# Queueing the casts of B and C behind bank copies, and taking two token tiles of the second layer by turns

## The chip, the cores and the metric

The kernel runs on one core of a Trainium2 chip. The metric is the device time of one execution in microseconds (us). Before the change the median of three runs is 602.65 us (601.85 to 606.14). The engines in the text are PE (TensorE, the matrix engine), ACT (ScalarE), DVE (VectorE), POOL (GpSimd) and SP (SyncE, which here only issues DMAs).

## The reference

```
# attention scan: batch 4, 8 heads, 768 positions, head dim 32, state 16
L = exp(cum[i] - cum[j]) * causal           # decay inside a chunk
y = ((C B^T) * L) x + decayed C state       # chunk by chunk, the state carried on
x = y as 3072 tokens x 256
# first layer, d_ff 768
h = max(x @ w1, x @ w2, x @ w3);  x = h @ w_out
# second layer, d_ff 1536
out = (sigmoid(x @ w_gate) * (x @ w_val)) @ w_out
```

x, a, B and C are 32-bit; the weights of both layers are 64-bit floating-point numbers that arrive as integer words and are turned into a hi/lo pair of 32-bit numbers on the chip ("decode").

## The kernel before, in words

**Tiling.** The 3072 tokens are 6 token tiles of 512 (t = 0 to 5). Each of the two layers goes through the tiles, and inside a tile through pieces of 128 hidden columns: 6 (m) in the first layer, 12 in the second. One piece of the first layer is three products `u` (one PSUM bank each, 6 matmuls of 128x512: two k, three terms of a hi/lo split), then the down product `o` of the piece before (6 matmuls into two banks). A piece of the second layer has two products `u` (gate and value) and the down product. So a tile of the first layer is 6 x (18 + 6) = 144 such matmuls and a tile of the second 12 x (12 + 6) = 216. The `u` banks rotate through three PSUM buffers (pool `psu`); a bank is free again when ACT or DVE has read it. In the first layer ACT copies bank 0 (`s`, line 383) and DVE takes the maximum with banks 1 and 2 (385, 387); then ACT casts `hi` (376) and POOL forms `lo` (378). In the second layer ACT forms the sigmoid (392), DVE the product with the value bank (394), ACT `hi`, and POOL (tile 0) or DVE (later tiles) `lo`.

**The attention runs ahead of the first layer.** It is cut into 8 chunks of 96 positions (c), each of 8 steps (g); a step is 4 small products `s` (C times B), a mask by the decay `dec` (`mt`), and 4 products `y`. Its steps are mixed into the first layer's slots (a slot is one `u` bank or one down product): while tile t runs, the steps that tile t + 1 needs are issued: 12 during tile 0, 8 during tile 1, 12 during tile 2, 12 during tile 3, 8 during tile 4, none during tile 5.

**B and C of a chunk** (`split_bc`, for chunks 2 to 7) are loaded as fp32 (`bc`), and split into three bf16 parts p = 0, 1, 2: ACT casts (`parts`, line 239), POOL subtracts (248), and after each cast SP issues DMAs (244; 6, 4 and 2 of them) that copy the part into `bi` and `cs`, from which PE reads. `bc` and `parts` have one buffer each, `bi` and `cs` two. `split_bc(c + 1)` is added to the pipe at the first step of chunk c.

**Weights of the second layer** are decoded in 24 pieces (two for each m: gate and value, 128x512; down, 128x256) during and after tile 5 of the first layer: three ACT operations (136, 138, 139), two on DVE (142, 144), a cast on ACT (148) and a subtraction on POOL (150). `weights_tick` starts one piece in each slot.

**What sets the order.** The code adds work in generators that advance by one stage at each tick, but the tile framework's scheduler then orders the instructions of each engine by its own estimate of when they are ready, so that an instruction can stand earlier in its engine's queue than the code has it. `tc.issue_after(i)` adds an edge for the order alone: what is traced inside it stands behind `i` in that engine's queue, with no wait for `i` to end. Every engine takes its queue in order.

## Time and profile before

| What | Value |
|---|---|
| Median of three runs | 602.65 us (601.85 to 606.14) |
| The profiled execution's own time, its span | 604.28 us, 602.5 us |
| PE busy | 563.0 us, 93% of the span |
| DVE, ACT, POOL busy | 53%, 43%, 31% |
| Last matmul of a `u` or `o` bank ends | about 599 us |

The profile is of one execution. Times inside it count from the span's start. PE's busy time contains overlap: one 128x512 matmul is shown with a length of 389 ns, while in a full stretch the next one starts after some 227 ns; so a tile's length says more than the busy share. A row of a timeline ends with the idle time ahead of the instruction and with what ended it, in brackets.

### The profile page before, as it was taken

To read this page: it belongs to the slowest core of one execution; us is meant where nothing else is said; L and a number is where in the kernel's file an instruction comes from. 1 tells how busy PE (TensorE), PEld (TensorE's weight loads), DVE (VectorE), ACT (ScalarE), POOL (GpSimd) and SP (SyncE) were. 2 spreads that over 40 slices of the span, in tenths; PEclk is the share of its full clock that TensorE was granted. 3 is DMA by queue.
4 is the path that set the end of the run, shared out by engine and by line. 5 is a ranking of instruction groups with operands and counts; after the bars stand their busy time and mean duration, and the time that the engine had idled before them with its cause. 6 is when DMAs were issued, how large, how long until landed. Compare 5 with 4: busy or idle time off the path is not lost.

```text
span 602.5 us, 8006 instructions
## 1 busy us (share of the span) xinstructions
PE 563.0 (93%) x2992; PEld 444.7 (74%) x2992; DVE 317.5 (53%) x467; ACT 260.0 (43%) x475; POOL 186.0 (31%) x207
## 2 busy tenths in 40 slices
PE   5778797997989999999999999999999999999997
PEld 4656575675767777777768888888888888888885
DVE  4899962644745755368987133344344334334332
ACT  5777653224233223279897243233233223223322
POOL 3668874335453424237668210000000000000000
PEclk9859998998999989999999999999999999999999
DMA  7998975373763900099000000000000000000000
GB/s 252 326 313 233 205 183 93 102 132 86 155 134 83 178 28 1 1 316 312 1 2 0 2 35 1 0 1 35 2 0 36 0 1 36 1 1 35 1 0 35
DMA packets 35367, 50.53 MB, mean 84 GB/s; under 512 B 3456, under 2 KB 24320, under 8 KB 35328
## 3 DMA queue, kind: packets, MB, share of 16 engines
q1 hardware_dynamic: 35328, 50.02, 32.0%
q8 instruction: 23, 0.38, 0.3%
q14 instruction: 16, 0.13, 0.1%
HBM read 38.51 MB, written 3.25 MB: 69 GB/s over the span
## 4 chain that ended last, share of the span: by engine, by line
PE 63%; DVE 9%; DMA 8%; ACT 5%; issue 4%; POOL 2%; SPq 1%; DVEq 0%; ACTq 0%; POOLq 0%
PE u L338 14%; PE u L339 14%; PE u L340 14%; PE o L339 7%; PE o L340 6%; PE o L338 6%; DMA cs<-parts 4%; DVE dec L228 2%; DMA dec<-ad 1%; DMA bc<-in_bch 1%; DVE t_b L142 1%; DVE s L387 1%; DVE s L385 1%; PE y L291 1%; POOL lo L378 1%
## 5 line engine op out<-in xcount | busy, mean ns | idle before, releaser
L376 ACT CAST hi<-s 128x512 fp32r<-128x512 f32 x108 | 67.1, 621 | 193.1 <-DVE s L394 153.8
L394 DVE TENSOR_TENSOR s<-u,s 128x512 f32<-128x512 f32 x72 | 49.7, 690 | 126.2 <-PE u L340 125.9
L338 PE MATMUL u<-xt_hi,w_b 128*128 128x512 f32 x288 | 112.4, 390 | 0.8 <-DVE s L385 0.6
L339 PE MATMUL u<-xt_lo,w_b 128*128 128x512 f32 x288 | 112.1, 389 | 0.0
L340 PE MATMUL u<-xt_hi,w_b 128*128 128x512 f32 x288 | 112.1, 389 | 0.0
L338 PE MATMUL u<-xt_hi,w_a 128*128 128x512 f32 x216 | 90.8, 420 | 10.4 <-ACT s L383 5.8
L339 PE MATMUL u<-xt_lo,w_a 128*128 128x512 f32 x216 | 87.2, 404 | 1.8 <-DVE xt_lo L302 1.8
L340 PE MATMUL u<-xt_hi,w_a 128*128 128x512 f32 x216 | 87.0, 403 | 0.0
L378 POOL TENSOR_TENSOR lo<-s,hi 128x512 fp32r<-128x512 f32 x48 | 66.4, 1384 | 64.1 <-ACT hi L376 63.0
L338 PEld LDWEIGHTS u<-xt_hi,w_b 128*128 128x128 f32 x288 | 54.1, 188 | 13.3 <-DVE s L385 1.1
L378 DVE TENSOR_TENSOR lo<-s,hi 128x512 fp32r<-128x512 f32 x60 | 41.5, 692 | 40.6 <-ACT hi L376 40.4
L340 PEld LDWEIGHTS u<-xt_hi,w_b 128*128 128x128 f32 x288 | 54.1, 188 | 11.3
L339 PEld LDWEIGHTS u<-xt_lo,w_b 128*128 128x128 f32 x288 | 54.1, 188 | 11.0
L338 PEld LDWEIGHTS u<-xt_hi,w_a 128*128 128x128 f32 x216 | 42.2, 195 | 25.1 <-ACT s L383 8.0
L228 DVE TENSOR_TENSOR_SCAN dec<-dec,delta 128x388 f32<-128x388 f32 x64 | 57.9, 944 | 3.2 <-DMA dec<-ad 3.0
L339 PE MATMUL o<-lo,w_b 128*128 128x512 f32 x144 | 56.1, 390 | 0.0
L340 PE MATMUL o<-hi,w_b 128*128 128x512 f32 x144 | 56.0, 389 | 0.0
L339 PEld LDWEIGHTS u<-xt_lo,w_a 128*128 128x128 f32 x216 | 42.1, 195 | 10.3 <-DVE xt_lo L302 2.3
L340 PEld LDWEIGHTS u<-xt_hi,w_a 128*128 128x128 f32 x216 | 42.0, 194 | 9.5
L392 ACT ACTIVATE s<-u 128x512 f32<-128x512 f32 x72 | 43.2, 600 | 10.8 <-PE u L340 9.8
L385 DVE TENSOR_TENSOR s<-u,s 128x512 f32<-128x512 f32 x36 | 24.6, 685 | 40.4 <-PE u L340 25.8
L338 PE MATMUL o<-hi,w_b 128*128 128x512 f32 x144 | 45.3, 390 | 0.5 <-ACT hi L376 0.5
(60 smaller groups left out, 761.6 us busy)
## 6 DMA issues: line engine op xcount, KB each, us to landing
dec<-ad SPq DMA_DIRECT2D x30, 388.0 KB, 5.6
raw_a<-in_w SPq DMA_DIRECT2D x18, 256.0 KB, 6.2
bi<-parts SPq DMA_DIRECT2D x36, 128.0 KB, 6.7
cs<-parts SPq DMA_DIRECT2D x36, 96.0 KB, 6.8
xs<-in_xh SPq DMA_DIRECT2D x6, 512.0 KB, 7.1
raw_b<-in_wg SPq DMA_DIRECT2D x12, 256.0 KB, 5.8
raw_b<-in_wv SPq DMA_DIRECT2D x12, 256.0 KB, 5.8
raw_b<-in_wo SPq DMA_DIRECT2D x12, 256.0 KB, 5.8
```

The costliest lines, as they stand in the source:

```text
L142: dve.scalar_tensor_tensor(out=t, in0=f1, scalar=3, in1=sg, op0=ALU.logical_shift_left, op1=ALU.bitwise_or)
L228: dve.tensor_tensor_scan(out=f, data0=f, data1=delta.rearrange("p u w -> p (u w)"), initial=0.0, op0=ALU.mult, op1=ALU.add)
L291: pe.matmul(y[32 * q:32 * q + 32, g % 4, 0:CH + N], xs[c][:, 4 * g + q, :], m[:, q, :], start=True, stop=True)
L338: pe.matmul(ps, wlo, a_hi(k), start=k == 0, stop=False)
L339: pe.matmul(ps, whi, a_lo(k), start=False, stop=False)
L340: pe.matmul(ps, whi, a_hi(k), start=False, stop=k == kn - 1)
L376: act.copy(hl[0], s)
L378: eng.tensor_tensor(out=hl[1], in0=s, in1=hl[0].bitcast(F32), op=ALU.subtract)
L385: dve.tensor_tensor(out=s, in0=banks[1], in1=s, op=ALU.max)
L387: dve.tensor_tensor(out=s, in0=banks[2], in1=s, op=ALU.max)
L392: act.activation(out=s, in_=banks[0], func=AF.Sigmoid)
L394: dve.tensor_tensor(out=s, in0=banks[1], in1=s, op=ALU.mult)
```

## The change

Three edits, and the tables that go with them.

First, the casts of B and C for chunks 3 to 7 are traced behind `evict[0]`, ACT's latest read of a `u` bank, and the split is taken forward by one part at each step of the attention (`prepare`), where it went forward by one part at each tick. Second, tiles 0 and 1 of the second layer alternate piece by piece, with a second pair of banks for the down product (`psos`, in the banks that the attention has given up); the `lo` of both tiles is formed on POOL. Third, the decode of the second layer's weights starts one piece in every third slot, and its ACT and DVE operations are queued behind the latest bank read of their engine. The split of the first layer's output for tiles 0 and 1 is made in pieces 2 and 4 of tile 5.

```diff
--- before.py
+++ after.py
@@ -129,29 +129,36 @@
 
     def decode(raw, wpool, blocks, name):
         nb = raw.shape[1]
+
+        def behind(k):
+            return tc.issue_after(evict[k].ins) if name[0] == "b" else ExitStack()
+
         f1 = raw[..., 1]
         r = stp.tile([128, DEC // 128, 128], I32, tag="r", bufs=3, name=f"r_{name}")[:, 0:nb]
         sg = sgs[len(blocks_done) % len(sgs)][:, 0:nb]
         blocks_done.append(name)
-        act.activation(out=sg.bitcast(F16).rearrange("p b (n t) -> p b n t", t=2)[..., 1], in_=f1.bitcast(F32),
-                       func=AF.Identity, scale=2.0 ** -112)
-        act.mul(f1.bitcast(F32), f1.bitcast(F32), 2.0 ** -112)
-        act.mul(r, raw[..., 0].bitcast(U32), 2.0 ** -29)
+        with behind(0):
+            act.activation(out=sg.bitcast(F16).rearrange("p b (n t) -> p b n t", t=2)[..., 1], in_=f1.bitcast(F32),
+                           func=AF.Identity, scale=2.0 ** -112)
+            act.mul(f1.bitcast(F32), f1.bitcast(F32), 2.0 ** -112)
+            act.mul(r, raw[..., 0].bitcast(U32), 2.0 ** -29)
         yield
         t = stp.tile([128, DEC // 128, 128], I32, tag="t", bufs=2, name=f"t_{name}")[:, 0:nb]
-        dve.scalar_tensor_tensor(out=t, in0=f1, scalar=3, in1=sg, op0=ALU.logical_shift_left,
-                                 op1=ALU.bitwise_or)
-        dve.tensor_tensor(out=r, in0=t, in1=r, op=ALU.add)
+        with behind(1):
+            dve.scalar_tensor_tensor(out=t, in0=f1, scalar=3, in1=sg, op0=ALU.logical_shift_left,
+                                     op1=ALU.bitwise_or)
+            dve.tensor_tensor(out=r, in0=t, in1=r, op=ALU.add)
         yield
         w = wpool.tile([128, 2, nb, 128], F32R, tag=name, name=f"w_{name}")
         blocks += [(w[:, 0, b], w[:, 1, b]) for b in range(nb)]
-        act.copy(w[:, 0], r.bitcast(F32))
+        with behind(0):
+            act.copy(w[:, 0], r.bitcast(F32))
         yield
         pool.tensor_tensor(out=w[:, 1], in0=r.bitcast(F32), in1=w[:, 0].bitcast(F32),
                            op=ALU.subtract)
 
-    def weights_tick():
-        if loaded:
+    def weights_tick(last=True):
+        if loaded and last:
             pipe.add(decode(*loaded.pop(0)))
 
 
@@ -236,7 +243,8 @@
         cs[c] = awk.tile([KT, NU, CH], BF16, tag="cs", name=f"cs{c}")
         yield
         for p in range(3):
-            act.copy(parts[:, p], r)
+            with tc.issue_after(evict[0].ins) if c > 2 else ExitStack():
+                act.copy(parts[:, p], r)
             for k, (dst, cols) in enumerate(((bi[c % 2], slice(0, BW)),
                                              (cs[c], slice(BW, BW + 384)))):
                 for t, pr in enumerate(TERMS):
@@ -246,10 +254,12 @@
                             in_=parts[:, p, cols])
             if p < 2:
                 pool.tensor_tensor(out=r, in0=r, in1=parts[:, p], op=ALU.subtract)
-                yield
+            yield splits if p == 2 else None
 
     steps = [(c, g) for c in range(NC) for g in range(NG)]
     done = [0]
+    evict = [None, None]
+    splits = []
     last = [None]
 
     def need(t):
@@ -313,7 +323,9 @@
         c, g = divmod(k, NG)
         if g == 0 and 0 < c < NC - 1:
             load_x(c + 1)
-            pipe.add(split_bc(c + 1))
+            splits.append(split_bc(c + 1))
+        if splits and next(splits[0], None) is splits:
+            splits.pop()
         n = k // 2
         if k % 2 == 0:
             if 5 <= n + 4 < NC * NP:
@@ -343,13 +355,13 @@
 
     def down(t, m, mn, w, hl, finish):
         if m == 0:
-            acc[0] = [pso.tile([128, TT], F32, tag=f"o{d}", name=f"o{mn}_{t}_{d}")
+            acc[t] = [psos[t % len(psos)].tile([128, TT], F32, tag=f"o{d}", name=f"o{mn}_{t}_{d}")
                       for d in range(KD)]
         first = len(w) - KD
         for d in range(KD):
-            three(acc[0][d], [m], mn, w, lambda k: first + d, lambda k: hl[0], lambda k: hl[1])
+            three(acc[t][d], [m], mn, w, lambda k: first + d, lambda k: hl[0], lambda k: hl[1])
         if m == mn - 1:
-            pipe.add(finish(t, acc[0]))
+            pipe.add(finish(t, acc[t]))
 
     def finish1(t, ps):
         yield
@@ -380,18 +392,18 @@
     def most(s, banks, hl):
 
         yield
-        act.copy(s, banks[0])
+        evict[0] = act.copy(s, banks[0])
         yield
         dve.tensor_tensor(out=s, in0=banks[1], in1=s, op=ALU.max)
         yield
-        dve.tensor_tensor(out=s, in0=banks[2], in1=s, op=ALU.max)
+        evict[1] = dve.tensor_tensor(out=s, in0=banks[2], in1=s, op=ALU.max)
         yield from hidden(s, hl, pool)
 
     def gated(s, banks, hl, eng):
         yield
-        act.activation(out=s, in_=banks[0], func=AF.Sigmoid)
-        yield
-        dve.tensor_tensor(out=s, in0=banks[1], in1=s, op=ALU.mult)
+        evict[0] = act.activation(out=s, in_=banks[0], func=AF.Sigmoid)
+        yield
+        evict[1] = dve.tensor_tensor(out=s, in0=banks[1], in1=s, op=ALU.mult)
         yield from hidden(s, hl, eng)
 
     chain = Pipe()
@@ -446,7 +458,7 @@
 
     slots = 4 * M1
     slot = 0
-    wp2 = []
+    wp2, psos = [], [pso]
     pend = None
 
     def slot_end():
@@ -457,7 +469,7 @@
                 for _ in range(2 if t > 1 else 1):
                     att_step(1 if t > 1 else 0)
         tick()
-        weights_tick()
+        weights_tick(t < NTT - 1 or s % 3 == 2)
 
     for t in range(NTT):
         for m in range(M1):
@@ -472,25 +484,29 @@
             if t == NTT - 1 and m == 0:
                 actx.close()
                 wp2.append(ctx.enter_context(tc.tile_pool(name="wp2", bufs=1)))
+                psos.append(ctx.enter_context(tc.tile_pool(name="pso2", bufs=1, space=PSUM)))
                 todo += [(piece2, m, part) for m in range(M2) for part in range(2)]
                 while todo:
                     load_weights()
-            if t == NTT - 1 and m == 3:
-                pipe.add(split_y(0))
-
-
-    for t in range(NTT):
-        for m in range(M2):
-            eng = pool if t == 0 else dve
-            for hl in layer(t, m, wt2[m], 2, lambda s, b, h: gated(s, b, h, eng)):
-                tick()
-                weights_tick()
-            if m == 6 and t + 1 < NTT:
-                pipe.add(split_y(t + 1))
-            down(*pend)
+            if t == NTT - 1 and m in (2, 4):
+                pipe.add(split_y(m // 2 - 1))
+
+
+    order = [(t, m) for m in range(M2) for t in range(2)]
+    order += [(t, m) for t in range(2, NTT) for m in range(M2)]
+    for t, m in order:
+        eng = pool if t < 2 else dve
+        for hl in layer(t, m, wt2[m], 2, lambda s, b, h: gated(s, b, h, eng)):
             tick()
-            weights_tick()
-            pend = (t, m, M2, wt2[m], hl, finish2)
+            slot += 1
+            weights_tick(slot % 3 == 2)
+        if m == 6 and 0 < t < NTT - 1:
+            pipe.add(split_y(t + 1))
+        down(*pend)
+        tick()
+        slot += 1
+        weights_tick(slot % 3 == 2)
+        pend = (t, m, M2, wt2[m], hl, finish2)
     for _ in range(2):
         tick()
     down(*pend)
```

Where the instructions go, in three places. Names carry numbers: `u_2_0_0` is tile 2, piece 0, bank 0; `parts_1630` reads `bc_1630`; lines from 139 on stand 7 to 12 lower in the changed file.

ACT at the start of tile 2 of the first layer, before; the casts are those of chunk 6, the `mt` copies those of chunk 4:

```order
L376 CAST hi_1_5_1271<-s_1_5_1270 128x512
L239 CAST parts_1632<-bc_1630 128x896
L383 COPY s_2_0_1310<-u_2_0_0_1313 128x512
L281 COPY mt_100<-s_0_1321 128x4x96
L357 COPY y_91<-o_1_0_1082 128x512
L357 COPY y_91<-o_1_1_1083 128x512
L239 CAST parts_1632<-bc_1630 128x896
L281 COPY mt_102<-s_2_1380 128x4x96
L376 CAST hi_2_0_1311<-s_2_0_1310 128x512
L239 CAST parts_1632<-bc_1630 128x896
L383 COPY s_2_1_1390<-u_2_1_0_1393 128x512
```

And now, where the casts are those of chunk 5:

```order
L388 CAST hi_1_5_1271<-s_1_5_1270 128x512
L395 COPY s_2_0_1310<-u_2_0_0_1313 128x512
L247 CAST parts_1357<-bc_1355 128x896
L291 COPY mt_100<-s_0_1321 128x4x96
L369 COPY y_91<-o_1_0_1079 128x512
L369 COPY y_91<-o_1_1_1080 128x512
L291 COPY mt_102<-s_2_1388 128x4x96
L388 CAST hi_2_0_1311<-s_2_0_1310 128x512
L395 COPY s_2_1_1398<-u_2_1_0_1401 128x512
L247 CAST parts_1357<-bc_1355 128x896
L388 CAST hi_2_1_1399<-s_2_1_1398 128x512
L247 CAST parts_1357<-bc_1355 128x896
```

The first cast stood ahead of the copy of bank `u_2_0_0` and stands behind it now. The casts of a chunk have moved later as well: those of chunk 4 from pieces 4 and 5 of tile 0 to pieces 0 and 1 of tile 1, those of chunk 5 from the start of tile 1 to here, those of chunk 6 from here to pieces 3 and 4 of tile 2, those of chunk 7 from there to pieces 1 and 2 of tile 3.

SP around the transfers of chunk 5 (`parts_1378` before, `parts_1357` now), before:

```order
L234 DMA bc_1376<-in_bch 128x896
L206 DMA dec_983<-ad 128x776
L234 DMA bc_1630<-in_bch 128x896
L206 DMA dec_1068<-ad 128x776
L217 DMA bx_1352<-in_bn 128x512
L206 DMA dec_1141<-ad 128x776
L244 DMA bi_97<-parts_1378 16x8x512
L206 DMA dec_1215<-ad 128x776
L244 DMA bi_97<-parts_1378 16x8x512 x2
L244 DMA cs_1379<-parts_1378 16x8x384 x2
```

And now:

```order
L241 DMA bc_1355<-in_bch 128x896
L224 DMA bx_1352<-in_bn 128x512
L213 DMA dec_1141<-ad 128x776
L213 DMA dec_1215<-ad 128x776
L224 DMA xs_1351<-in_xh 128x1024
L252 DMA bi_97<-parts_1357 16x8x512 x3
L252 DMA cs_1358<-parts_1357 16x8x384 x2
L213 DMA dec_1359<-ad 128x776
```

The load of chunk 6 (`bc_1630`) no longer stands ahead of chunk 5's transfers, and two loads of the decay and one of x have gone ahead of them.

ACT in the second layer, at pieces 1 and 2 of tile 0, before (`sg`, `raw_b`, `r_b` and `w_b` are the decode):

```order
L392 ACTIVATE s_0_1_3009<-u_0_1_0_3012 128x512
L138 ACTIVATE raw_b_2574<-raw_b_2574 128x512
L139 ACTIVATE r_b_2948<-raw_b_2574 128x512
L376 CAST hi_0_0_2953<-s_0_0_2952 128x512
L357 COPY y_91<-o_5_0_2630 128x512
L136 ACTIVATE sg_88<-raw_b_2577 128x256
L357 COPY y_91<-o_5_1_2631 128x512
L148 CAST w_b_2964<-r_b_2931 128x256
L139 ACTIVATE r_b_2969<-raw_b_2577 128x256
L136 ACTIVATE sg_87<-raw_b_2579 128x512
L376 CAST hi_0_1_3010<-s_0_1_3009 128x512
```

And now, at piece 1 of tiles 0 and 1:

```order
L404 ACTIVATE s_0_1_2921<-u_0_1_0_2924 128x512
L141 ACTIVATE sg_88<-raw_b_2555 128x256
L144 ACTIVATE r_b_2956<-raw_b_2555 128x256
L155 CAST w_b_2944<-r_b_2917 128x512
L143 ACTIVATE raw_b_2555<-raw_b_2555 128x256
L388 CAST hi_0_1_2922<-s_0_1_2921 128x512
L404 ACTIVATE s_1_1_2960<-u_1_1_0_2963 128x512
L155 CAST w_b_2983<-r_b_2956 128x256
L141 ACTIVATE sg_87<-raw_b_2557 128x512
L144 ACTIVATE r_b_2993<-raw_b_2557 128x512
L143 ACTIVATE raw_b_2557<-raw_b_2557 128x512
L388 CAST hi_1_1_2961<-s_1_1_2960 128x512
```

One decode of three operations and one cast stands between a sigmoid and its `hi` now, where up to six operations of the decode and the copies stood before; the decode goes on until piece 8.

## Rows read from the trace of the kernel before

**Rows 1.** By token tile: us, PE, PEld, DVE, ACT, POOL busy (count), PEclk, DMA.
```profile
34.20:86.69 52.49, 45.23 (x295) 33.92 (x295) 49.60 (x73) 35.64 (x62) 42.09 (x40) 0.92 0.94 236
86.69:133.63 46.94, 43.26 (x246) 30.65 (x244) 21.37 (x36) 13.55 (x24) 17.37 (x21) 0.93 0.56 114
133.63:182.25 48.62, 42.07 (x290) 31.50 (x289) 26.11 (x44) 16.65 (x29) 23.99 (x28) 0.96 0.58 123
182.25:225.87 43.62, 41.52 (x290) 31.77 (x288) 28.05 (x47) 13.63 (x26) 16.52 (x24) 0.96 0.49 99
225.87:263.66 37.79, 37.79 (x241) 28.77 (x239) 15.05 (x24) 13.07 (x26) 12.71 (x14) 1.00 0.18 54
263.66:299.29 35.63, 34.41 (x145) 26.63 (x145) 33.27 (x42) 33.46 (x71) 24.70 (x19) 1.00 0.62 209
299.29:350.00 50.71, 49.08 (x211) 38.98 (x210) 28.75 (x35) 33.07 (x67) 29.67 (x24) 1.00 0.00 1
350.00:398.96 48.96, 48.96 (x217) 40.54 (x216) 18.40 (x27) 16.18 (x28) 1.56 (x1) 1.00 0.03 11
```

**Rows 2.** What PE waited for, 94 to 133 us: total us, times, longest.
```profile
PE o L338 <- ACT hi L376: 2.5, 1, 2.5
PE o L339 <- POOL lo L378: 1.2, 1, 1.2
```

**Rows 3.** Timeline of ACT, 88 to 104 us: start, length, operation, [idle <-ended by].
```profile
98.28 0.94 ACT L239 CAST parts<-bc 128x896 bf16<-128x896 f32 x1 [9.06 <-DMA bc<-in_bch]
```

**Rows 4.** What PE waited for, 133 to 182.25 us.
```profile
PE u L338 <- ACT s L383: 5.3, 2, 3.8
PE o L339 <- POOL lo L378: 0.8, 1, 0.8
```

**Rows 5.** Timeline of ACT, 130 to 143 us.
```profile
139.30 0.94 ACT L239 CAST parts<-bc 128x896 bf16<-128x896 f32 x1 [5.43 <-DMA cs<-parts]
```

**Rows 6.** Timeline of ACT, 160 to 188 us.
```profile
174.07 0.94 ACT L239 CAST parts<-bc 128x896 bf16<-128x896 f32 x1 [5.85 <-DMA cs<-parts]
```

**Rows 7.** What PE waited for, 182.25 to 226 us.
```profile
PE s L273 <- DVE s L385: 1.2, 1, 1.2
PE u L338 <- DVE s L387: 0.5, 1, 0.5
```

**Rows 8.** Timeline of DVE, 205 to 214 us.
```profile
207.44 1.81 DVE L228 TENSOR_TENSOR_SCAN dec<-dec,delta 128x388 f32<-128x388 f32 x2 [1.22 <-DMA dec<-ad]
```

**Rows 9.** Two stretches in the columns of rows 1; PEclk is the 0.50.
```profile
100.20:107.00 6.80, 5.52 (x12) 3.71 (x12) 0.69 (x1) 3.25 (x6) 5.52 (x6) 0.50 0.04 5
141.20:144.60 3.40, 3.40 (x10) 2.62 (x9) 0.69 (x1) 1.81 (x3) 3.40 (x4) 0.50 0.11 27
```

**Rows 10.** Timeline of PE, 88 to 104 us: one step's `s`, one step's `y`.
```profile
95.52 0.34 PE L273 MATMUL s<-cs,bi 96*128 96x96 bf16 x4
95.80 0.40 PE L291 MATMUL y<-mt,xs 128*32 128x112 f32 x8
96.13 0.50 PE L338 MATMUL u<-xt_hi,w_a 128*128 128x512 f32 x1
```

**Rows 11.** Instructions on `bc`: duration ns min/median/max, first and last start us.
```profile
L239 ACT CAST parts<-bc x18: 921/938/942, 19.1 to 180.0; 128x896 bf16<-128x896 f32 x18
L248 POOL TENSOR_TENSOR bc<-bc,parts x12: 1887/1900/2351, 20.1 to 178.0; 128x896 f32<-128x896 f32 x12
```

**Rows 12.** Instructions on `cs`: issues (ns), landing of their transfers (us).
```profile
L244 SPq DMA_DIRECT2D cs<-parts x36: 547/597/1571, 26.7 to 200.6; - x36
...
DMA to landing us min/median/max: 5.2/6.8/9.3
```

**Rows 13.** The page by line: count | busy us, mean ns | idle us.
```profile
L385 DVE TENSOR_TENSOR s<-u,s 128x512 f32<-128x512 f32 x36 | 24.6, 685 | 40.4 <-PE u L340 25.8
```

**Rows 14.** Timeline of POOL, 318 to 332 us.
```profile
317.99 1.84 POOL L378 TENSOR_TENSOR lo<-s,hi 128x512 fp32r<-128x512 f32 x1 [1.04 <-ACT hi L376]
319.79 2.37 POOL L150 TENSOR_TENSOR w_b<-r_b,w_b 128x256 fp32r<-128x256 f32 x2
```

## The prediction

> **What bounds the kernel now.** I read the busy times by stretch first, one stretch for each token tile [rows 1]. Their edges are the starts of the tiles' first products `u`, counted off in the timeline. The last row is the second layer's tile 1: PE is busy in all of its 48.96 us, and 216 matmuls of 128x512 stand in it (12 x 18 by the code), so one takes 0.227 us. PE sets the time there, and in the tiles after it, which do the same work. What can be won lies ahead: a first-layer tile holds 144 such matmuls, 32.6 us, and the tiles took 52.5, 46.9, 48.6, 43.6, 37.8 and 35.6 us.
>
> Part of that is the attention's own work on PE. One step of it costs 0.28 us for `s` and 0.33 us for `y`, the distances between the starts in [rows 10], 0.61 us together. Tile 4 carries 8 steps, took 37.79 us and shows no idle PE, so I take it as what a tile with 8 steps costs when nothing is late; a tile with 12 steps would be 4 x 0.61 = 2.4 us longer, 40.2 us. By that, tile 1 (8 steps) has 9.2 us to win, tile 2 (12 steps) 8.4 and tile 3 (12 steps) 3.4, together 21.0 us. Tile 0 lost more than any, but there DVE is busy for 49.6 of 52.5 us, and the change takes next to nothing from DVE in that stretch.
>
> Then I read who was waited for. In tile 1 PE waited 2.5 us for a cast `hi` and 1.2 us for a `lo` [rows 2]; the timeline of ACT shows why: a cast of `parts` stood at the head of ACT's queue for 9.06 us, waiting for the load of `bc`, and `hi` stood behind it [rows 3]. In tile 2 PE waited 3.8 us for the copy `s` of a bank [rows 4]; it stood behind a cast that waited 5.43 us for the transfers of the chunk before to leave the one buffer of `parts` [rows 5]. The same happens again at 174 us, 5.85 us [rows 6], which gives the other 1.5 us of that wait and the `lo` after it. In tile 3 PE waited 1.7 us for DVE [rows 7], which had waited for a load of the decay [rows 8]. Three of these four places run into a stretch at half the clock, 1.2 instead of 2.4 GHz, in which PE does half of what it could: 6.8 us from 100.2, 3.4 us from 141.2, and another like that from 212.9 [rows 9].
>
> **The change, part by part.** *Casts behind bank copies.* Nothing is added or removed: 15 of 18 casts move, with their 10 subtractions on POOL and 60 transfers. In front of each copy or `hi` that was late stood a cast that was not ready; now the copy goes first. What each place gives back:
>
> - tile 1: 2.5 + 1.2 us of waiting and half of 6.8 us at half clock [rows 2, 9], 7.1 us
> - tile 2, first place: 3.8 + 1.7 = 5.5 us [rows 4, 9]
> - tile 2, second place: 1.5 + 0.8 = 2.3 us [rows 4, 6]
> - tile 3: 1.2 + 0.5 + 1.7 = 3.4 us [rows 7, 9]
>
> That is 18.3 us, below the 21.0 us of the other reckoning, as it has to be. Not all of it need come. The place in tile 3 hangs on a load of the decay, which stood on SP behind transfers of `bi` and `cs`; it stands behind six of them and a load of x still, and starts earlier only as far as these do. Its bounds are 0 and 3.4 us; I take the middle, 1.7.
>
> Later casts mean later transfers. Between the copies that the last two casts of a chunk stand behind and the first `s` that reads them, the new order on PE has 48 large matmuls, four `s` and four `y` for chunk 5: 48 x 0.227 + 4 x 0.61 = 13.3 us. For chunks 4, 6 and 7 there are over 20 us. The way for chunk 5: the last cast stands behind `hi` of the same piece, which waits for two more banks (2.7 us), DVE's maximum (0.69 us [rows 13]) and itself, a narrower cast than the 0.94 us of [rows 11], so 4.3 us at most; the cast is 0.94 us; two issues of SP are 0.6 us each, and landing takes 6.8 us, 5.2 to 9.3 [rows 12]. Sum 13.2 us, 11.6 to 15.7. The subtraction of 1.90 us [rows 11] lies beside the wait for `hi`. So chunk 5 arrives between 1.7 us early and 2.4 us late; I charge 1.2 us, the middle of 0 and 2.4, and no fall of the clock. The Trainium skill's page "DMA: Bandwidth & Descriptors", section "Anatomy of one DMA", gives some 2.0 us fixed plus the bytes at 436 GB/s for the software-driven path; by it the transfers of 96 KB would land in about 2.2 us, and that charge would be nothing, for a sum larger by 1.2 us. The rows measure three times as much, so I go by them.
>
> *The second layer's start.* Tile 5 of the first layer took 35.63 us against 32.6 of work, and tile 0 of the second 50.71 against 48.96 [rows 1]: 3.0 + 1.75 = 4.7 us is all there is. ACT is busy for 33.46 of the 35.63 us; over these two stretches it works 66.5 of 86.3 us. The same decode now ends some 48 us later, and with the next tile's own 16.2 us ACT has 82.7 us of work in 135 us, 61%. A piece starts every 3 slots, two pieces for each m, and m takes six slots with two tiles in turn: supply equals demand, with seven pieces ahead from tile 5, so weights aren't late. The `lo` of tile 1 moves to POOL, 12 of them; POOL was idle in that tile but for 1.56 us. I take 4.0 of the 4.7 us and leave one wait like the 0.8 us of [rows 4], since the first pieces of the second layer still have decode in the way. The bounds are 0 and 4.7. The second pair of banks for `o` and the table of slots cost no instruction.
>
> **Sum.** 18.3 - 1.7 - 1.2 + 4.0 = 19.4 us. The profiled execution took 604.28 us, with a span of 602.5 and 1.8 us around it; 584.9 us is left. It lay 1.6 us above the median of the runs, 602.65, so in the measure of the runs I predict 583.
>
> **The rivals.** *The waits change their names (0.20).* An engine's queue that no longer blocks lets PE run faster into whatever is late next: loads of the decay, and the parts of chunk 5 with a fall of the clock behind them. For it: chunk 5 has no margin at the median landing, and the load of [rows 8], whose place on SP is hardly better. Against it: tile 4, with the same engines and 8 steps, shows nothing late [rows 1]. If half of the 18.3 us comes back so, the gain is 9.2 + 4.0 less 1.7 us for one more fall of the clock [rows 9], 11.5, and the time 591.
>
> *Everything goes (0.10).* The tiles come down to tile 4's pace and the second layer's start to its work: 21.0 + 4.7 = 25.7 us, 577.
>
> *Only the second layer gains (0.07).* The casts hold up ACT at their new places as they did at the old ones, now because the last cast of a chunk waits for POOL's subtraction in front of the next copy. For it: three casts of a chunk still share one `bc` and one `parts`. Against it: the chunk before has 9 us or more to leave the buffer. Then 602.65 - 4.0 = 598.7, within 1%.
>
> *Slower (0.04).* POOL becomes the bound of the alternating stretch. In each of its 24 steps of 18 matmuls, 4.08 us, POOL forms one `lo`, up to 1.84 us, and a half decode of 1.19 us at the least (two took 2.37) [rows 14]. If `lo` came late by one such decode in every step, PE would lose 24 x 1.19 = 28.6 us, and the time be 612. It decides from 19.4 / 24 = 0.81 us of lateness on. The Trainium skill's "GPSIMD Engine Reference", section "Key points", says that POOL shares its SBUF interfaces with DVE instructions that read two inputs there, as two of the decode's do. Against it: in tile 0 of the second layer the same `lo` stood beside a decode twice as dense, and the tile lost 1.75 us [rows 1]; and the new order on PE has the down product two pieces behind its `u`, 34 matmuls or 7.7 us after the gate bank.
>
> **Numbers.** The forecast has 0.59. Its own range is 578 to 589: the unknown terms are 0 to 3.4 for tile 3, 0 to 2.4 for chunk 5, 0 to 4.7 for the second layer. To hold 8 in 10 I go from 577, less 1 for the spread of the runs, up to 595, through the first rival with a second fall of the clock; the last two rivals stay out. One per cent, about what a measurement of this kernel can tell from no change, is 6.0 us. Faster by that: 0.59 + 0.10 + most of 0.20, 0.87. Within it: 0.07 + 0.02, 0.09. Slower: 0.04.
>
> **What would show it.** Right: the tiles 1, 2 and 3 of the first layer at 40, 41 and 42 us; no cast of `parts` with over 2 us of idle time ahead of it while a copy of a bank is due; PE at the full clock from about 110 us to the end, or but one fall; tile 5 near 33.5 us and the two tiles in turn near 98.5 us together. Wrong: PE waiting at `s` for DMA of `cs` or `bi` in tile 2; DVE waiting for the decay in tiles 2 and 3; PE waiting for `lo` from POOL in the alternating stretch; tile 0 of the first layer longer than 52.5 us, which I took as it was.

## The result, and the profile after

The changed kernel takes 582.08 us, median of four runs (581.04 to 582.93); the kernel before took 604.39 us beside it (601.85 to 606.48). The ratio is 0.9632, 95% interval 0.9583 to 0.9681. In a second series it was 0.9622 (0.9582 to 0.9662), 580.86 us. 583 was forecast, 576 to 595.

The profiled execution took 582.93 us with a span of 581.1, against 602.5 before: 21.4 us less. First the page, engine by engine (busy us, share of the span, instructions), and the granted clock in 40 slices:

```profile
PE 560.9 (97%) x2992; PEld 448.7 (77%) x2992; DVE 312.7 (54%) x455; ACT 260.7 (45%) x475; POOL 197.8 (34%) x219
...
PEclk9998999999999999999999999999999999999999
```

PE is busy for 97% of the span. The last slice under 9 is the fourth; the fall in it, in the columns of [rows 1], PEclk 0.50:

```profile
49.70:53.10 3.40, 3.10 (x14) 2.29 (x15) 3.40 (x5) 2.66 (x5) 2.89 (x3) 0.50 1.13 245
```

Now the stretches that answer to [rows 1], each from the first `u` of a tile to that of the next; the last two are the first and the second half of the stretch in which two tiles of the second layer go by turns:

```profile
38.19:91.95 53.76, 47.53 (x298) 34.77 (x299) 49.74 (x71) 33.28 (x59) 38.28 (x38) 0.97 0.89 220
91.95:130.16 38.21, 38.21 (x238) 27.77 (x237) 20.92 (x36) 13.34 (x23) 17.37 (x20) 1.00 0.56 111
130.16:171.12 40.96, 40.67 (x293) 31.40 (x292) 26.93 (x46) 17.38 (x30) 24.06 (x28) 1.00 0.85 172
171.12:211.14 40.02, 39.58 (x289) 30.61 (x288) 27.27 (x46) 15.89 (x29) 20.29 (x26) 1.00 0.52 111
211.14:248.78 37.64, 37.64 (x242) 28.96 (x241) 16.20 (x25) 12.16 (x23) 12.73 (x14) 1.00 0.18 54
248.78:281.42 32.64, 32.64 (x146) 27.03 (x145) 15.82 (x26) 20.66 (x42) 14.22 (x11) 1.00 0.68 229
281.42:329.01 47.59, 47.59 (x211) 39.41 (x210) 34.14 (x38) 35.70 (x73) 28.45 (x24) 1.00 0.00 1
329.01:377.98 48.97, 48.97 (x218) 40.54 (x217) 23.56 (x29) 27.42 (x53) 23.18 (x20) 1.00 0.00 1
```

Against [rows 1]: tiles 1, 2 and 3 are 8.7, 7.7 and 3.6 us shorter, tile 4 is 0.2 shorter, and from the start of tile 5 to the last matmul it takes 328.6 us instead of 335.1, 6.5 less. That is 26.6 us; 5.3 us are lost again ahead of tile 1, which starts at 91.95 instead of 86.69. From tile 1 on the clock is 1.00 in every stretch.

Then what PE still waited for between 92 and 211 us, where [rows 2, 4, 7] add up to 11.5 us:

```profile
PE u L350 <- DVE s L399: 0.4, 1, 0.4
PE s L283 <- DVE s L397: 0.3, 1, 0.3
```

Neither `ACT s` nor `ACT hi` nor `POOL lo` is among them, and from 211 us to the end the list is empty. ACT at the start of tile 2, the place of [rows 5] (start, length, operation, [idle before <- ended by]):

```profile
131.72 0.59 ACT L395 COPY s<-u 128x512 f32<-128x512 f32 x1 [0.41 <-PE u L352]
132.20 0.94 ACT L247 CAST parts<-bc 128x896 bf16<-128x896 f32 x1
...
139.63 0.59 ACT L395 COPY s<-u 128x512 f32<-128x512 f32 x1 [1.05 <-PE u L352]
140.11 0.94 ACT L247 CAST parts<-bc 128x896 bf16<-128x896 f32 x1
...
143.66 0.94 ACT L247 CAST parts<-bc 128x896 bf16<-128x896 f32 x1
```

The copy goes first and waits only for its own bank. The cast behind it starts without an idle moment, where it had held the queue for 5.43 us. Of the 15 casts that moved, one waits longer than 1 us: 1.75 us, for POOL's subtraction.

### The profile page after: what moved, and what is told of

Read it like the earlier page. It is cut to its first block, busy times and chain, and to the rows that moved or that the text cites. A ratio compares the mean times of both kernels' runs of the same rounds, so it can differ in the third digit from the quotient of the medians.

```text
span 581.1 us, 8016 instructions
## 1 busy us (share of the span) xinstructions
PE 560.9 (97%) x2992; PEld 448.7 (77%) x2992; DVE 312.7 (54%) x455; ACT 260.7 (45%) x475; POOL 197.8 (34%) x219
## 4 chain that ended last, share of the span: by engine, by line
PE 87%; DMA 6%; DVE 3%; issue 1%; SPq 1%; ACT 1%; POOL 0%; DVEq 0%; ACTq 0%; POOLq 0%
PE u L350 19%; PE u L351 18%; PE u L352 18%; PE o L351 8%; PE o L350 8%; PE o L352 8%; PE s L280 3%; PE y L301 3%; DMA raw_a<-in_w 3%; PE s L283 1%; DMA dec<-in_ah 1%; DMA cs<-parts 1%; DMA raw_a<-in_wo 1%; DVE dec L235 1%; SPq L252 0%
## 5 line engine op out<-in xcount | busy, mean ns | idle before, releaser
L390 POOL TENSOR_TENSOR lo<-s,hi 128x512 fp32r<-128x512 f32 x60 | 80.9, 1348 | 95.3 <-ACT hi L388 92.3
L350 PE MATMUL u<-xt_hi,w_a 128*128 128x512 f32 x216 | 89.1, 413 | 2.9 <-DVE s L399 2.0
L351 PE MATMUL u<-xt_lo,w_a 128*128 128x512 f32 x216 | 85.5, 396 | 0.1
L352 PE MATMUL u<-xt_hi,w_a 128*128 128x512 f32 x216 | 85.0, 394 | 0.0
L350 PEld LDWEIGHTS u<-xt_hi,w_a 128*128 128x128 f32 x216 | 41.2, 191 | 14.7 <-DVE s L399 2.5
L390 DVE TENSOR_TENSOR lo<-s,hi 128x512 fp32r<-128x512 f32 x48 | 33.2, 692 | 32.5 <-ACT hi L388 32.4
L352 PEld LDWEIGHTS u<-xt_hi,w_a 128*128 128x128 f32 x216 | 41.1, 190 | 9.1
```

The lines of the kernel that those rows point to most:

```text
L350: pe.matmul(ps, wlo, a_hi(k), start=k == 0, stop=False)
L351: pe.matmul(ps, whi, a_lo(k), start=False, stop=False)
L352: pe.matmul(ps, whi, a_hi(k), start=False, stop=k == kn - 1)
L390: eng.tensor_tensor(out=hl[1], in0=s, in1=hl[0].bitcast(F32), op=ALU.subtract)
```

## The experiments

**The two halves apart.** The first kernel is the kernel before with the casts' part of the change alone (the order edge, and the pace at which the work of a chunk goes forward); the second is the changed kernel with that part undone.

```diff
 kernel before
-            act.copy(parts[:, p], r)
+            with tc.issue_after(evict[0].ins) if c > 2 else ExitStack():
+                act.copy(parts[:, p], r)
...
-                yield
+            yield splits if p == 2 else None
...
-            pipe.add(split_bc(c + 1))
+            splits.append(split_bc(c + 1))
+        if splits and next(splits[0], None) is splits:
+            splits.pop()
```

> The casts of B and C alone are changed (order edge and one part per attention step); the second layer is as before. Theory (the two halves of the change are independent, and add): tiles 1, 2 and 3 of the first layer take 38.2, 41.0 and 40.0 us as in the changed kernel, 20.0 us less than before, tile 5 and the second layer as before; time 584 to 589 us, 14 to 20 less. Rival (part of the gain of the casts needs the freer second layer, or the head really gets longer by 5 us with them): 590 to 595 us.

> The second layer's part alone (tiles 0 and 1 by turns, a piece of the decode in every third slot behind bank reads); B and C are cast as before. Theory: from the start of tile 5 on 6.5 us less, tiles 1 to 3 as before; 597 to 600 us. Rival (what is saved there is lost elsewhere, as the stalls ahead only end later): 601 to 605 us.

> The changed kernel itself, as the one to compare with. Expected 0.963 of the time before, and 581 to 583 us. In its first profile the stretch ahead of tile 1 of the first layer was 5.3 us longer than before (91.95 against 86.69 us), with the small fp32 products at half clock from about 11 us on. Theory: that is a matter of the single execution, and a second profile can have tile 1 begin 3 to 5 us earlier. Rival: the new order does it, and tile 1 begins at 91 to 93 us again.

Measured: casts alone 587.36 us, ratio 0.9728 (0.9687 to 0.977); second layer alone 596.39, 0.9873 (0.9829 to 0.9917); both, run again, 580.86. The kernel before took 602.47 beside them. The gains are 15.1, 6.1 and 21.6 us: within the intervals they add up, so neither half lives on the other. The stretches of the casts alone, tiles 1, 2, 3 and 5 and the second layer's tile 0:

```profile
89.51:127.71 38.20, 38.20 (x238) 27.76 (x237) 20.93 (x36) 13.29 (x23) 17.39 (x20) 1.00 0.55 111
127.71:168.70 40.99, 40.70 (x294) 31.41 (x292) 26.94 (x46) 17.36 (x30) 24.06 (x28) 1.00 0.86 171
168.70:208.73 40.03, 39.59 (x290) 30.61 (x289) 27.28 (x46) 15.88 (x29) 20.31 (x26) 1.00 0.52 112
...
246.51:282.14 35.63, 34.43 (x146) 26.60 (x146) 33.32 (x42) 33.44 (x71) 24.74 (x19) 1.00 0.63 210
282.14:332.84 50.70, 49.04 (x212) 38.98 (x210) 28.71 (x35) 33.02 (x67) 29.64 (x24) 1.00 0.00 1
```

The first three are those of the changed kernel to 0.03 us, the last two those of before. With the second layer alone it is the other way round; what PE waited for there in tiles 1 to 3, and its tile 5 and the stretch after it:

```profile
PE u L347 <- ACT s L392: 5.3, 2, 4.2
PE o L348 <- POOL lo L387: 2.8, 3, 1.5
```

```profile
259.22:291.86 32.64, 32.64 (x146) 27.03 (x145) 15.82 (x26) 20.64 (x42) 14.22 (x11) 1.00 0.67 225
291.86:339.46 47.60, 47.60 (x212) 39.41 (x211) 34.53 (x38) 35.66 (x73) 28.50 (x24) 1.00 0.00 1
```

**Edge or pace.** The casts' part has two pieces: the edge that puts a cast behind a bank copy, and the pace, by which a split goes forward by one part at each step of the attention and not at each tick. Each alone, on the kernel before:

```diff
 edge alone
-            act.copy(parts[:, p], r)
+            with tc.issue_after(evict[0].ins) if c > 2 else ExitStack():
+                act.copy(parts[:, p], r)
...
 pace alone
-                yield
+            yield splits if p == 2 else None
...
-            pipe.add(split_bc(c + 1))
+            splits.append(split_bc(c + 1))
+        if splits and next(splits[0], None) is splits:
+            splits.pop()
```

> Of the first half only the pace is changed: the split of B and C goes forward by one part at each attention step in place of each tick, with no order edge; the second layer is as before. Theory: the order edge does it, and without it the scheduler puts the casts where they stood, so tiles 1 to 3 wait as before: 600 to 606 us. Rival (the later pace is what helps): 584 to 592 us.

> Of the first half only the order edge is taken: casts of chunks 3 to 7 behind the latest read of a bank, but the split goes forward by one part at each tick as before; the second layer is as before. Theory (the edge does it, the pace adds nothing): 585 to 589 us, as with both (587.4). Rival (the pace is needed so that a cast finds its part subtracted, and ACT waits less): 590 to 598 us.

Measured: the pace alone 605.37 us, ratio 1.0051 (1.0015 to 1.0086); the edge alone 585.56, 0.972 (0.9675 to 0.9766). The edge is all of the gain. With it alone this is all that PE waited for between 88 and 222 us:

```profile
PE s L276 <- DVE s L388: 0.3, 1, 0.3
```

ACT with the pace alone, the first cast of chunks 5, 6 and 7:

```profile
100.03 0.94 ACT L239 CAST parts<-bc 128x896 bf16<-128x896 f32 x1 [5.77 <-DMA bc<-in_bch]
...
139.40 0.94 ACT L239 CAST parts<-bc 128x896 bf16<-128x896 f32 x1 [5.88 <-DMA cs<-parts]
...
175.20 0.94 ACT L239 CAST parts<-bc 128x896 bf16<-128x896 f32 x1 [6.37 <-DMA cs<-parts]
```

These are the waits of [rows 3, 5, 6] again, and PE waited 6.3 us for `ACT s` with them. The Trainium skill's page "PSUM — Partial Sum Buffer", section "Engine vs sequencer instructions", says that ScalarE's queue is strictly first in, first out; the rows agree.

**More buffers instead of another order.** [Rows 5] names the one buffer of `parts` as what the cast waited for. So I gave it a second one, and then `bc` a second one as well, in the kernel before:

```diff
-        parts = awk.tile([128, 3, BW + 384], BF16, tag="parts", bufs=1, name=f"parts{c}")
+        parts = awk.tile([128, 3, BW + 384], BF16, tag="parts", bufs=2, name=f"parts{c}")
 and, in the second of the two
-        r = awk.tile([128, BW + 384], F32, tag="bc", bufs=1, name=f"bc{c}")
+        r = awk.tile([128, BW + 384], F32, tag="bc", bufs=2, name=f"bc{c}")
```

> The kernel before with two buffers for parts in place of one, and nothing else. A cast then need not wait for the transfers of the chunk before. Theory (the waits of casts at the head of ACT's queue cost the time): no cast waits for DMA of cs any more, the 4 us wait of PE in tile 2 and the one at its end go, while the cast that waits for the load of bc stays: tile 2 at 41 to 44 us, time 592 to 598. Rival (it is the casts' place ahead of bank copies that costs, whether they wait or not): tile 2 at 47 us or over, 600 to 605.

> As the one before, and two buffers for bc as well, so that a cast need not wait for its load either. Theory: the wait of 9 us for bc goes too; tiles 1 to 3 at 38 to 41 us, time 586 to 590, as with the order edge, if the scheduler's earlier casts don't load tile 0, where DVE is full, by more than 2 us. Rival (casts that come early wait for the next thing, POOL's subtraction or the free bi): tile 1 or 2 stays above 44 us, 594 to 602.

> The kernel before once more, for its head alone. Theory: whether PE's clock rises at 11 us or only at 43 us is a matter of the execution: tile 0 of the first layer can begin at 34 or at 38 us, and the clock may or may not fall after the waits of tiles 1 to 3; tile 1 between 86 and 91 us, tile 1's length 42 to 47. Rival (the order of the kernel before sets it): tile 0 at 34.2 us again, tiles 1 to 3 at 46.9, 48.6 and 43.6 us within 0.5.

Measured: two `parts` 599.61 us, ratio 0.9953 (0.9924 to 0.9982); two of both 602.73, 1.0015 (0.998 to 1.0051); the kernel before against itself 602.80, 1.0011 (0.9973 to 1.0048). Both are slower than the theory had them (592 to 598, and 586 to 590): the buffers don't cure it. Casts of the first, then of the second:

```profile
98.86 0.94 ACT L239 CAST parts<-bc 128x896 bf16<-128x896 f32 x1 [7.76 <-issue]
...
140.22 0.94 ACT L239 CAST parts<-bc 128x896 bf16<-128x896 f32 x1 [6.24 <-DMA cs<-parts]
```

```profile
103.12 0.94 ACT L239 CAST parts<-bc 128x896 bf16<-128x896 f32 x1 [6.54 <-DMA bc<-in_bch]
...
144.56 0.94 ACT L239 CAST parts<-bc 128x896 bf16<-128x896 f32 x1 [4.95 <-DMA cs<-parts]
```

The waits are as long as before. With a buffer free the order on ACT has the casts of the next chunks earlier still (with two `parts` nine casts run between 98 and 148 us, and those of chunk 7 among them), so the last of them meets the same wait for transfers that are still under way. What holds PE up is a cast queued ahead of its data, whatever the number of buffers. But the buffers do move something. With two of both, tiles 1 to 3 took 130.9 us together, against 136.4 in the second profile of the kernel before, and tile 0 lost as much, which no run takes apart. Tile 0 in that profile of the kernel before, then with two of both, in the columns of [rows 1]:

```profile
37.38:88.57 51.19, 45.07 (x294) 33.83 (x295) 48.34 (x71) 35.74 (x62) 42.39 (x40) 0.93 0.89 226
```

```profile
37.89:94.43 56.54, 48.84 (x295) 35.86 (x295) 47.99 (x71) 35.73 (x62) 41.96 (x40) 0.94 0.83 222
```

Whether buffers together with an order that spares tile 0 would do as well as the edge, no run shows.

**How much margin is left.** The forecast charged 1.2 us for transfers of chunk 5 that arrive late. In the changed kernel the last of them landed at 150.2 us and the first `s` that reads it started at 152.56, so 2.4 us were left. One step later they should be late:

```diff
 changed kernel, in the function that splits a chunk
         yield
+        yield
         for p in range(3):
```

> The changed kernel with the casts of every chunk one attention step later. In the changed kernel the last transfer of chunk 5 landed 2.3 us ahead of its first use, those of the others 12 to 23 us. Theory (landing is the next thing late): the last cast of chunk 5 moves by about 3.5 us, PE waits some 1 to 2 us at its s, and the clock may fall after it (1.7 us more): 582.5 to 586 us. Rival (casts back to back hold up ACT, whatever the transfers do): PE waits for s or hi from ACT in tiles 2 and 3, and over 586 us.

Measured: 580.54 us, ratio 0.9652 (0.959 to 0.9714), no other than the changed kernel, where 582.5 to 586 was expected. PE at that `s`:

```profile
151.83 0.50 PE L284 MATMUL s<-cs,bi 96*128 96x96 bf16 x8 [1.81 <-DMA dec<-ad]
```

The wait is there. The row names a load of the decay, but the last transfer of `cs` landed at 151.7 us, just ahead of the start. Tile 2 took 41.37 us instead of 40.96 for it, tile 3 40.73 instead of 40.02, tile 1 37.84 instead of 38.21, and the clock did not fall. (The sum counts, not the tile: four `o` moved from tile 2 into tile 3.) So the margin is real, and a wait of 1.8 us past it costs some 0.7 us over the three tiles, which the times cannot tell from nothing.

**Turns and spacing of the decode.** Two more kernels take the second layer's part apart. The first keeps the turns, but gives the decode every slot and no edge, as before; the second keeps spacing (every second slot) and edges, and does tile after tile.

```diff
 turns alone (changed kernel)
-            return tc.issue_after(evict[k].ins) if name[0] == "b" else ExitStack()
+            return ExitStack()
...
-        weights_tick(t < NTT - 1 or s % 3 == 2)
+        weights_tick()
...
-            weights_tick(slot % 3 == 2)
+            weights_tick()
 spacing and edges, no turns (changed kernel)
-        weights_tick(t < NTT - 1 or s % 3 == 2)
+        weights_tick(t < NTT - 1 or s % 2 == 1)
...
-    order = [(t, m) for m in range(M2) for t in range(2)]
-    order += [(t, m) for t in range(2, NTT) for m in range(M2)]
+    order = [(t, m) for t in range(NTT) for m in range(M2)]
...
-        eng = pool if t < 2 else dve
+        eng = pool if t < 1 else dve
...
-            weights_tick(slot % 3 == 2)
+            weights_tick(slot % 2 == 1)
```

> The changed kernel, but with one piece of the decode in every slot and no order edge on it: tiles 0 and 1 of the second layer by turns are all that is left of that half. Theory (the crowded decode on ACT and DVE is what cost the time around the layers' border, not the order of the tiles): tile 5 takes 35 to 36 us again and the time is 3 to 6 us over the changed kernel, 585 to 588. Rival (taking turns is what helps): within 1 us of the changed kernel, 581 to 583.

> The changed kernel, but the second layer's tiles one after the other as before, and one piece of the decode in every second slot (with the order edges), which is as slow as the weights allow without turns. Theory: spreading is what counts, and a half slower decode gets most of it: 582 to 584 us, tile 5 at 32.7 to 33.5 us. Rival (turns are needed, as ACT and DVE are too full for tile 0 at this pace): 585 to 588 us.

Measured: turns alone 587.64 us, ratio 0.9754 (0.9691 to 0.9816), the casts' gain and nothing more; spacing without turns 584.74, 0.971 (0.9659 to 0.9761). Tile 5 and the first stretch of the second layer, with turns alone and then with spacing and no turns:

```profile
249.08:284.72 35.64, 34.54 (x146) 26.56 (x146) 33.30 (x42) 33.45 (x71) 24.68 (x19) 1.00 0.63 212
284.72:336.23 51.51, 49.38 (x211) 38.95 (x210) 29.24 (x36) 32.55 (x66) 29.58 (x24) 1.00 0.00 1
```

```profile
246.40:279.04 32.64, 32.64 (x145) 27.03 (x144) 21.02 (x30) 22.95 (x48) 16.74 (x14) 1.00 0.69 230
279.04:330.57 51.53, 49.70 (x211) 38.87 (x210) 38.61 (x47) 45.30 (x93) 35.80 (x29) 1.00 0.00 1
```

Spacing and its edges together give all of tile 5's 3.0 us; which of the two does it, no run shows. In the stretch after it the decode has to go somewhere: in one tile's time ACT then works 45.30 of 51.53 us and PE loses 3.9 us against the 47.6 of the changed kernel. Only with the turns, which double the time until the next weights are wanted, are both stretches free of waits. The parts of this half depend on each other, where the halves did not.

**POOL or DVE for the second tile's `lo`.**

```diff
-        eng = pool if t < 2 else dve
+        eng = pool if t < 1 else dve
```

> The changed kernel, but with the 12 lo of the second layer's tile 1 on DVE in place of POOL. Theory: off the path, as PE waits for nothing from tile 5 on: the same within 1 us, 581 to 583. Rival (POOL is near its limit in the alternating stretch, hidden by a little): 1 to 3 us faster; or DVE is, and it is slower by as much.

Measured: 580.34 us, ratio 0.9635 (0.9583 to 0.9687), the same, with the same 96.56 us for the two tiles together. The rival with POOL as the bound is dead from both sides: PE waited for no `lo` in the changed kernel, and taking 12 of them from POOL brings nothing.

## Why the prediction held, step by step

The time was right and the mechanism too: the copies were late because casts without data stood ahead of them. Several sizes were off, and they cancelled in part, so that 583 came this near is partly luck. By its own three terms the range should read 580 to 590 (gains of 23.0 down to 12.5 us) and not 578 to 589; the measured time lies in both.

- **Tiles 1 and 2: right.** Of the 8.7 us of tile 1, 1.8 are not a gain: its stretch holds eight `o` matmuls fewer (x238 against x246, at 0.227 us), four of which now lie in tile 0 and four in tile 2 (by name, 26 became 30 there, and 36 became 40). That leaves 6.9 us, 7.1 were forecast. Tile 2 gained 7.7 with those four in it, 8.6 without; 5.5 + 2.3 = 7.8 were forecast. Tile 2 is now at the pace of tile 4 and tile 1 is some 1.4 us short of it, so "the other reckoning", the upper bound of 21.0 us, was nearly reached: 6.9 + 8.6 + 3.6 = 19.1.
- **Tile 3: half of it was struck off, wrongly.** It gained 3.6 us; 3.4 stood in the sum, and 1.7 were taken off since the decay's load "starts earlier only as far as these do". No operation of DVE waits for the decay in tiles 1 to 3 any more. In the kernel before, the load of [rows 8] was issued at 199.41 us behind ten transfers of chunk 7, which had started only at 190.05 us, when PE's `s` had freed their buffer, and it landed 8.0 us later; in the changed kernel the loads of the decay from 182 us on land in 6.9 us at most. That late casts had held these transfers up, the rows do not show, so why the load now comes in time stays open. Of the 3.4 us, 1.7 stood for a fall of the clock at 212.9 us that is not among [rows 9] but is there, in the same columns:

```profile
212.90:216.30 3.40, 3.40 (x10) 2.66 (x9) 1.70 (x2) 0.81 (x2) 1.53 (x2) 0.50 0.38 117
```

- **Chunk 5: a charge that did not come.** 1.2 us were charged for a landing of 6.8 us; it was 5.2 us in the changed kernel, where [rows 12] give 6.8:

```profile
DMA to landing us min/median/max: 4.0/5.2/8.9
```

  Chunk 5 came 2.4 us early, past the best end of the range (1.7). Landings need not be that long: the stores of the second layer's output, where the page's DMA row stands at a tenth or less, are larger and land in 2.1 us.

```profile
out_t<-ob SPq DMA_DIRECT2D x12, 256.0 KB, 2.1
```

  Both landings of `cs` lie well above the 2.2 us that the prediction estimated by the Trainium skill's page "DMA: Bandwidth & Descriptors", section "Anatomy of one DMA"; that section is on the software-driven path, and the queue here is a hardware one by the profile (`q1 hardware_dynamic`). Its result for this term, no charge, was nevertheless the one that came.
- **Second layer: too small, and so was its bound.** 6.5 us in the profiles and 6.1 in the times, where 4.0 were forecast and "4.7 us is all there is". The step that failed here is 50.71 against 48.96 in [rows 1]: the first stretch of the second layer holds six matmuls fewer than a full one, x211 against x217 in the same rows, so its work is 47.6 us and 3.1 us could be won there, not 1.75. With tile 5's 3.0 and 0.4 at the very end that is 6.5. All of it came.
- **Tile 0: a loss that was not in the sum.** The prediction took it "as it was". Two things happen ahead of tile 1. The first has nothing to do with the change: the matmuls of the head, the attention's steps ahead of tile 0, run at two speeds, by the execution. The group of `s<-y` from 11 to 34 us (count | busy us, mean ns | idle before), in the kernel before, in its second profile, and in the changed kernel:

```profile
L270 PE MATMUL s<-y 128*128 128x96 f32 x78 | 13.0, 321 | 4.3 <-ACT mt L281 3.2 <-DVE mt L285 1.1
```

```profile
L270 PE MATMUL s<-y 128*128 128x96 f32 x79 | 19.5, 432 | 0.0
```

```profile
L280 PE MATMUL s<-y 128*128 128x96 f32 x77 | 19.1, 432 | 0.6 <-DVE mt L295 0.6
```

  The kernel before starts tile 1 at 86.69 us in the one profile and at 88.57 in the other, so this is worth 1.9 us. The second thing is the change. Between executions with the same head, tile 1 starts at 88.57 before, and at 91.95 and 90.87 in two profiles of the changed kernel, 2.3 to 3.4 us later; 0.8 us of it is there already when tile 0 starts (37.38 against 38.19 and 38.18 us). The four `o` that moved in are 0.9 us of work, but with the pace alone they stay in tile 1, and tile 0 takes 53.00 us all the same, against 52.70 in the second profile of the changed kernel. In tile 0 DVE sets the time, and its `t_a` of the weight decode shows the rest: before, after, and after in the second profile (between 34 and 88 us):

```profile
L142 DVE SCALAR_TENSOR_TENSOR t_a<-raw_a,sg 128x512 int32<-128x512 int32 x10 | 9.7, 973 | 0.1
```

```profile
L148 DVE SCALAR_TENSOR_TENSOR t_a<-raw_a,sg 128x512 int32<-128x512 int32 x10 | 11.6, 1162 | 1.2 <-DMA cs<-parts 1.1
```

```profile
L148 DVE SCALAR_TENSOR_TENSOR t_a<-raw_a,sg 128x512 int32<-128x512 int32 x10 | 10.5, 1054 | 1.2 <-ACT raw_a L143 1.1
```

  Ten of them take 1.9 us more in the first profile, 0.8 in the second, and wait 1.1 us more in both. The wait is for ACT's `raw_a`, as the second row has it: in the first profile too it ends at 79.21 us, and `t_a` starts at 79.23. The 1.1 us between the two profiles is one `t_a` (1.77 us at 44.69 us, against 0.69 in the second) that met an operation of POOL. The prediction had moved the casts in tile 0 without asking what POOL would then do beside DVE there. The pace alone makes tile 1 start late as well (91.13 us), with 10.5 us of `t_a` and the same wait, so the edge is not its only cause; which of the moved operations does it, I did not try.

With the `o` counted as work where they lie, the sum for this pair of profiles is then 6.9 + 8.6 + 3.6 + 0.2 + 6.5 - (5.3 - 0.9) = 21.4 us, against a forecast of 7.1 + 7.8 + 1.7 - 1.2 + 4.0 = 19.4.

Of the rivals, "everything goes" (577) was nearly right in both places it spoke of and wrong in leaving tile 0 alone. "The waits change their names" did not happen: the one new wait of this size is 1.1 us of DVE's, for ACT. Of the marks, the tiles at 40, 41 and 42 us came out at 38.2, 41.0 and 40.0, tile 5 at 32.64 instead of 33.5, the two tiles in turn at 96.56 instead of 98.5; the last fall of the clock is at 49.7 us, before the 110 that were named. One of the marks that would show it wrong is there: tile 0 took 53.76 us, and 52.70 in the second profile, where the mark was 52.5 us. It was rightly chosen: taking tile 0 "as it was" is the other step that failed.

## What to carry to other kernels

Where an engine's queue shows a long idle time ahead of an instruction and another engine waits for the one behind it, change the order, not the buffers: here an edge behind the copy that was due gave 16.9 us, and a second buffer 2.9 us at the most, and with two of both the loss went into another tile. Before a stretch's length is compared with "a full stretch", compare their instruction counts; six matmuls too few hid 1.4 of the second layer's 6.5 us. And where work is moved out of the way of one engine, look at what it now stands beside: the stretch that is bound by DVE paid for it.

## What the runs showed of the hardware

- `t_a` on DVE takes 0.67 to 0.69 us where no operation of POOL on two inputs is under way when it starts. Where one is, `t_a` ends some 0.55 us after that operation has ended, so that the same shape took anything from 0.78 to 1.77 us in tile 0 of the two kernels: it waits for its turn, it is not slowed. Below, POOL's `lo` ends at 74.83 us, and `t_a` 0.56 us later. The same pair stands in the kernel before, at 69.35 and 69.55 us, with the same 1.64 us. Where `t_a` is not the later one, POOL waits: in the kernel before one pair starts together, and `lo` takes 1.82 us for the 1.29 that it takes alone. Before, then after:

```profile
76.03 1.82 POOL L378 TENSOR_TENSOR lo<-s,hi 128x512 fp32r<-128x512 f32 x1 [0.33 <-ACT hi L376]
...
76.04 0.67 DVE L142 SCALAR_TENSOR_TENSOR t_a<-raw_a,sg 128x512 int32<-128x512 int32 x1
```

```profile
73.54 1.29 POOL L390 TENSOR_TENSOR lo<-s,hi 128x512 fp32r<-128x512 f32 x1
...
73.74 1.65 DVE L148 SCALAR_TENSOR_TENSOR t_a<-raw_a,sg 128x512 int32<-128x512 int32 x1
```

  The Trainium skill's "GPSIMD Engine Reference", section "Key points", says that POOL shares its SBUF interfaces with DVE and that they contend when a DVE instruction reads two inputs there; these rows agree, and add that either side may be the one that waits.
- The clock does not fall after every wait of PE. The kernel before fell in both of its profiles after the waits of tiles 1, 2 and 3; with the second layer's part alone it fell in tile 2 only. In tile 1 PE waited 1.5 and 0.5 us there, and 1.5 and 0.6 us in the second profile of the kernel before: the one did not fall and took 42.99 us, the other fell at 102.5 us and took 44.51.
- In the head the clock column reads 1.00 in two of the three executions shown above, the very two in which the same matmuls take 432 instead of 321 ns on average. So in the head the column does not tell the two speeds apart; what sets them, the runs don't tell.
